# Grouped-query attention on one core: six of eight Q loads move from SyncE's queue to GpSimd's, in a pattern of outermost count 8

## The chip, the core and the metric

The kernel runs on one core of one Trainium2 chip. The core has a matmul engine (TensorE, PE in the profile), two elementwise engines (VectorE, DVE; ScalarE, ACT), GpSimd (POOL), a sequencer that mostly issues transfers (SyncE, SP), and 16 DMA engines that carry all transfers between the device's memory and the core's on-chip memory of 128 partitions. The metric is the device time of one execution in microseconds.

## The reference

```python
B, Hq, Hkv, Sq, Sk, D = 16, 32, 8, 16, 2048, 128        # all bf16
k = jnp.repeat(k, Hq // Hkv, axis=1)
v = jnp.repeat(v, Hq // Hkv, axis=1)
scores = jnp.einsum("bhqd,bhkd->bhqk", q, k) * D ** -0.5
p = _softmax(scores, axis=-1)
return jnp.einsum("bhqk,bhkd->bhqd", p, v)
```

Four query heads of 16 rows share one K/V head, so each of the 16 x 8 = 128 groups is a 64-row softmax attention over 2048 keys of length 128. K and V are 512 KB a group each, Q and the output 16 KB: nearly all bytes are K and V, and each is read once.

## The kernel before

**Tiling.** Two groups make a pair, so that 2 x 64 query rows fill the 128 partitions. There are NP = 64 pairs, and eight pairs make a Q chunk of 1024 rows (NQC = 8 chunks, 256 KB each). For each pair the kernel loads K (`load_k`, L163, 1 MB) and V (`load_v`, L170, 1 MB). VectorE transposes K in blocks (L291, two instructions a pair); TensorE forms the scores `S_ps` (L244); VectorE scales them into `Sneg` and takes the row minimum of the negated scores (L307); ScalarE takes the exponential into `P` with its row sum (L336); TensorE transposes `P` in two halves (L259) and ScalarE copies them out (L346); TensorE multiplies by V (L275, "PV"), and ScalarE scales by the reciprocal row sum (L356) into `Osb`, which is stored (`store`, L190).

**Q.** A chunk is loaded by `load_q` (L183) into one of NQ = 2 buffers `Qn`, with eight consecutive rows of Q in a partition: partition a holds rows 8a to 8a+7, 2 KB in a piece. TensorE transposes it in four parts (L227; the operation "QT" of its program), and ScalarE copies each part into `QT` (L326), where it also puts the 1024 columns back in the order of the rows: column 8a+j comes from partition a, place j. The four parts of chunk c+1 are placed in the programs behind pairs 8c+2 to 8c+5.

**Order and queues.** Every engine runs a list that is written out before (`pe_prog`, `act_prog`), with semaphores between engines. SP issues all transfers in one loop over t (L195): K of pair t, then Q of chunk c when t = max(0, 8c - QLEAD) with QLEAD = 7, then V of pair t - 4, then the output of pair t - 12. It waits for a free buffer before each: K has six buffers (`sem_kt`), V eight (`sem_pv`), and Q of chunk c waits (L186) until chunk c-2 has been transposed (`sem_st`). The last pair's V is loaded in two halves (L181), and the second half of its PV waits for the second. GpSimd only builds the two identity matrices at the start, which TensorE waits for.

Of the kernel before, what the change touches and what calls it, by code (L numbers as in the profile page):

```python
# [5 lines left out]
ACT = mybir.ActivationFunctionType  # L6
ALU = mybir.AluOpType
BF16 = mybir.dt.bfloat16
# [8 lines left out]
NQ = 2  # L17
# [4 lines left out]
QLEAD = 7  # L22


def bass_standalone__gqa_softmax__sampling_kernel(
# [14 lines left out]
    NQC = NP // 8  # L40
# [3 lines left out]
    sb = lambda name, shape, dt: ctx.enter_context(nc.sbuf_tensor(name, shape, dt))  # L44
# [6 lines left out]
    Vb = [sb(f"Vb{i}", [128, 2, J, 128], BF16) for i in range(NV)]  # L51
    KT = [sb(f"KT{i}", [128, 2, J * 64], F32) for i in range(NKT)]
    Qn = [sb(f"Qn{i}", [128, 8, 128], BF16) for i in range(NQ)]

    QT = [sb(f"QT{i}", [128, 4, 1024], BF16) for i in range(2)]
    Sneg = [sb(f"Sneg{i}", [128, Sk], F32) for i in range(2)]
# [16 lines left out]
    sem_q = [sem(f"sem_q{i}") for i in range(NQ)]  # L73
    sem_o = [sem(f"sem_o{i}") for i in range(NO)]
    sem_kt = sem("sem_kt")
    sem_max = sem("sem_max")
    sem_rec = sem("sem_rec")
    sem_s = sem("sem_s")
# [61 lines left out]
    def stage_ap(u):  # L140
        return ST_ps[:, 512 * (u % NSTAGE):512 * (u % NSTAGE + 1)]
# [7 lines left out]
    with nc.Block() as block:  # L149

        @block.gpsimd
        def _(gp):
            gp.iota(iota_t[:, :], [[1, 128]], base=0, channel_multiplier=-1).then_inc(sem_id, 1)
            gp.wait_ge(sem_id, 1)
            gp.tensor_scalar(ident[:, :], iota_t[:, :], 0.0, None, op0=ALU.is_equal).then_inc(sem_id, 1)  # L155
            gp.tensor_scalar(ident4[:, :], iota_t[:, :], 0.0, None, op0=ALU.is_equal).then_inc(sem_id, 1)

        @block.sync
        def _(sp):
            def load_k(p):  # L160
                s = p % NK
                if p >= NK:
                    sp.wait_ge(sem_kt, 2 * (p - NK) + 2)  # L163
                if p == 0:
                    for g in range(2):
                        sp.dma_start(Kn[s][:, g, :], kf[:, g, :]).then_inc(sem_k0[g], 16)  # L166
                else:
                    sp.dma_start(Kn[s][:, :, :], kf[:, 2 * p:2 * p + 2, :]).then_inc(sem_k[s], 16)  # L168

            def load_v(p):  # L170
                s = p % NV
                if p >= NV:
                    sp.wait_ge(sem_pv, p - NV + 1)
                if p < NP - 1:
                    dst = Vb[s][:, :, :, :].rearrange("a g j d -> a g (j d)")
                    sp.dma_start(dst, vf[:, 2 * p:2 * p + 2, :]).then_inc(sem_v[s], 16)  # L176
                    return
                for x in range(2):
                    dst = Vb[s][:, :, 8 * x:8 * (x + 1), :].rearrange("a g j d -> a g (j d)")
                    src = vf[:, 2 * p:2 * p + 2, 1024 * x:1024 * (x + 1)]  # L180
                    sp.dma_start(dst, src).then_inc(sem_vl[x], 16)  # L181

            def load_q(c):  # L183
                s = c % NQ
                if c >= NQ:
                    sp.wait_ge(sem_st, last_q[c - NQ, 3] + 1)  # L186
                src = qf[1024 * c:1024 * (c + 1), :].rearrange("(a j) d -> a j d", j=8)
                sp.dma_start(Qn[s][:, :, :], src).then_inc(sem_q[s], 16)

            def store(p):  # L190
                s = p % NO
                sp.wait_ge(sem_nm, p + 1)
                sp.dma_start(of[128 * p:128 * (p + 1), :], Osb[s][:, :]).then_inc(sem_o[s], 16)  # L193

            for t in range(NP + SLAG + 1):  # L195
                if t < NP:
                    load_k(t)
                for c in range(NQC):
                    if t == max(0, 8 * c - QLEAD):
                        load_q(c)  # L200
                if 0 <= t - VLAG < NP:
                    load_v(t - VLAG)
                if 0 <= t - SLAG < NP:
                    store(t - SLAG)
            for s in range(NO):
                sp.wait_ge(sem_o[s], 16 * (NP // NO))

        @block.tensor
        def _(pe):
            pe.wait_ge(sem_id, 3)  # L210

            def free(u):
                if u >= NSTAGE:
                    pe.wait_ge(sem_ev, u - NSTAGE + 1)

            for op in pe_prog:
                if op[0] == "QT":
                    _, c, i, u = op
                    if i == 0:
                        pe.wait_ge(sem_q[c % NQ], 16 * (c // NQ + 1))  # L220
                    free(u)
                    dst = stage_ap(u).bitcast(BF16)
                    src = Qn[c % NQ][:, :, :].rearrange("p j (b c e) -> p j b e c", b=2, e=2)
                    b, e = divmod(i, 2)
                    for j in range(8):
                        for r in range(4):
                            ins = pe.transpose(dst[32 * r:32 * (r + 1), 128 * j:128 * (j + 1)], src[:, j, b, e, :], ident[:, :])  # L227
                    ins.then_inc(sem_st, 1)
                elif op[0] == "S":
                    _, p = op  # L230
                    pe.wait_ge(sem_kt, 2 * p + 2)
                    if p >= 1:
                        pe.wait_ge(sem_max, p)
                    c, i = divmod(p, 8)
                    if i == 0:
                        pe.wait_ge(sem_ev, last_q[c, 3] + 1)
                    kt = KT[p % NKT][:, :, :].bitcast(BF16).rearrange("p g (t b x e) -> p g b e t x", t=J // 2, b=2, e=2)
                    qt = QT[c % 2]
                    for acc in range(4):
                        b, e = divmod(acc, 2)  # L240
                        for r in range(4):
                            rows = slice(32 * r, 32 * (r + 1))
                            for g in range(2):
                                ins = pe.matmul(  # L244
                                    S_ps[64 * g:64 * (g + 1), 512 * r:512 * (r + 1)],
                                    qt[rows, acc, 128 * i + 64 * g:128 * i + 64 * (g + 1)],
                                    kt[rows, g, b, e, :, :],
                                    start=(acc == 0), stop=(acc == 3),
                                )
                    ins.then_inc(sem_s, 1)  # L250
                elif op[0] == "PT":
                    _, p, h, u = op
                    if h == 0:
                        pe.wait_ge(sem_exp, p + 1)
                    free(u)
                    dst = stage_ap(u)
                    for t in range(4):
                        x = 4 * h + t
                        ins = pe.transpose(dst[:, 128 * t:128 * (t + 1)], P[p % 2][:, 128 * x:128 * (x + 1)], ident4[:, :])  # L259
                    ins.then_inc(sem_st, 1)  # L260
                elif op[0] == "PV":
                    _, p = op
                    pe.wait_ge(sem_ev, last_p[p, 1] + 1)
                    if p < NP - 1:
                        pe.wait_ge(sem_v[p % NV], 16 * (p // NV + 1))
                    if p >= NP - 3:
                        pe.wait_ge(sem_max, NP)
                    elif p >= 1:
                        pe.wait_ge(sem_nm, p)
                    pt = PT[p % NPT][:, :, :].bitcast(BF16).rearrange("p t (q e) -> p t e q", e=2)  # L270
                    for j in range(J):
                        if p == NP - 1 and j % 8 == 0:
                            pe.wait_ge(sem_vl[j // 8], 16)
                        for g in range(2):
                            ins = pe.matmul(  # L275
                                o_ap(p)[64 * g:64 * (g + 1), :],
                                pt[:, j // 2, j % 2, 64 * g:64 * (g + 1)],
                                Vb[p % NV][:, g, j, :],
                                start=(j == 0), stop=(j == J - 1),
                                skip_group_check=True,  # L280
                            )
                    ins.then_inc(sem_pv, 1)
# [36 lines left out]
        def _(act):  # L319
            for op in act_prog:  # L320
                if op[0] == "qe":
                    _, c, i, u = op
                    act.wait_ge(sem_st, u + 1)
                    if c >= 2 and i == 0:
                        act.wait_ge(sem_s, 8 * (c - 1))
                    act.activation(  # L326
                        QT[c % 2][:, i, :].rearrange("p (a j) -> p a j", j=8),
                        stage_ap(u).bitcast(BF16).rearrange("p (j a) -> p a j", j=8), ACT.Copy,
                    ).then_inc(sem_ev, 1)
                elif op[0] == "exp":  # L330
                    _, p = op
                    act.wait_ge(sem_max, p + 1)
# [53 lines left out]
```

## Time and profile before

| what | value |
|---|---|
| median of three timed runs | 353.08 us (351.69 to 353.13) |
| the profiled execution, its time | 352.63 us |
| its span, first to last instruction | 350.4 us |
| mean granted TensorE clock | 0.937 |
| read from device memory, written | 136.31 MB, 2.10 MB |
| mean rate over the span | 395 GB/s |

In the page, "busy" is the time in which an engine executed, and its share is of the span. The strip of slices cuts the span into 40 and gives a digit for tenths. A group of instructions shows its line, engine, operation, tiles and count, then busy us, the mean ns of one, the idle time of the engine before the group's instructions, and what ended that idle time. The queue lines give packets, megabytes and the time their packets took as a share of all 16 DMA engines' span; a queue of kind "instruction" carries the engines' programs. A line of the answer by stretches gives the stretch and its length, then the busy time and count of PE, PEld (TensorE's weight loads), DVE, ACT and POOL, then the granted clock, the DMA share and the GB/s.

### The profile page before, as it was taken

The page shows a single profiled execution, that of the slowest core. Times are in us where ns is not written, and L with a number is a line of the kernel's source. Part 1 is how long each engine was busy: PE and PEld are TensorE (multiplying, and loading weights), DVE is VectorE, ACT ScalarE, POOL GpSimd, SP SyncE. Part 2 cuts the span into 40 slices and gives each one's busy share as a digit, 9 for nine tenths or more (in the row PEclk, how much of TensorE's full clock was granted, in tenths as well). Part 3 has the DMA queues.
Part 4 walks back from the last instruction along what each step waited for, and adds up shares of the span by engine and source line. Part 5 has one row for each costly group of instructions (what it writes and reads, how often), then busy time and mean ns, then how long its engine had stood idle before and what let it go on. Part 6 is the DMA issues. An engine that isn't in the chain of part 4 may idle for free.

```text
span 350.4 us, 12631 instructions
## 1 busy us (share of the span) xinstructions
PE 243.3 (69%) x5632; PEld 173.5 (50%) x5632; DVE 296.3 (85%) x320; ACT 255.6 (73%) x353; POOL 1.4 (0%) x7
## 2 busy tenths in 40 slices
PE   2578876778667775687649666676775776697675
PEld 2246544546445543365436544454563554465454
DVE  2899999978789887889888897898888888988980
ACT  2578887877758785678757976578957689676575
POOL 1000000000000000000000000000000000000000
PEclk9769999998989999899998999899988999988899
DMA  7999999999999999999999999999999999999983
GB/s 280 416 408 409 406 408 405 412 411 408 414 410 410 412 409 411 410 413 408 408 412 411 409 412 408 410 415 406 411 412 410 410 389 410 412 411 411 409 342 117
DMA packets 45525, 139.22 MB, mean 397 GB/s; under 512 B 11424, under 2 KB 11424, under 8 KB 45472
## 3 DMA queue, kind: packets, MB, share of 16 engines
q1 hardware_dynamic: 45472, 138.42, 99.5%
q8 instruction: 44, 0.72, 0.8%
q14 instruction: 9, 0.07, 0.1%
HBM read 136.31 MB, written 2.10 MB: 395 GB/s over the span
## 4 chain that ended last, share of the span: by engine, by line
DMA 75%; DVE 10%; SPq 6%; issue 5%; PE 2%; ACT 1%
DMA Kn<-in_k_dram 70%; DVE KT L291 8%; DMA Vb<-in_v_dram 4%; SPq L176 3%; DVE Sneg L307 2%; SPq L193 2%; DMA Qn<-in_q_dram 1%; ACT QT L326 1%; SPq L168 1%; PE S_ps L244 1%; PE O_ps L275 0%; PE ST_ps L227 0%; SPq L181 0%; SPq L166 0%; ACT O L356 0%
## 5 line engine op out<-in xcount | busy, mean ns | idle before, releaser
L291 DVE STREAM_TRANSPOSE KT<-Kn 128x1024 f32<-128x1024 f32 x128 | 151.8, 1225 | 43.6 <-DMA Kn<-in_k_dram 43.5
L336 ACT ACTIVATE P<-Sneg,nbias 128x2048 bf16<-128x2048 f32 x64 | 128.1, 2001 | 37.4 <-DVE Sneg L307 37.0
L307 DVE TENSOR_SCALAR_CACHE_REDUCE Sneg<-S_ps 128x2048 f32<-128x2048 f32 x64 | 144.2, 2253 | 1.8 <-PE S_ps L244 1.8
L244 PE MATMUL S_ps<-KT,QT 32*64 32x512 bf16 x2048 | 81.3, 425 | 87.5 <-DVE Sneg L307 75.2
L244 PEld LDWEIGHTS S_ps<-KT,QT 32*64 32x64 bf16 x2048 | 33.7, 109 | 113.5 <-issue 102.7
L346 ACT ACTIVATE PT<-ST_ps 128x512 f32<-128x512 f32 x128 | 69.9, 596 | 21.4 <-PE ST_ps L259 21.4
L259 PE MATMUL ST_ps<-ident,P 128*128 128x128 f32 x512 | 73.1, 288 | 8.9 <-ACT P L336 8.6
L275 PEld LDWEIGHTS O_ps<-Vb,PT 128*64 128x64 bf16 x1952 | 63.1, 119 | 30.3 <-issue 28.8
L275 PE MATMUL O_ps<-Vb,PT 128*64 128x128 bf16 x1952 | 73.7, 233 | 1.2 <-issue 1.0
L259 PEld LDWEIGHTS ST_ps<-ident,P 128*128 128x128 f32 x512 | 57.5, 145 | 18.1 <-ACT P L336 13.6
L356 ACT ACTIVATE O<-O_ps,rrec 128x128 bf16<-128x128 f32 x61 | 22.3, 366 | 25.7 <-PE O_ps L275 25.0
L326 ACT ACTIVATE QT<-ST_ps 128x1024 bf16<-128x1024 bf16 x32 | 32.4, 1024 | 5.6 <-PE ST_ps L227 5.5
L227 PE MATMUL ST_ps<-ident,Qn 128*32 128x128 bf16 x1024 | 21.4, 233 | 6.4 <-DMA Qn<-in_q_dram 6.4
L227 PEld LDWEIGHTS ST_ps<-ident,Qn 128*32 128x32 bf16 x1024 | 16.3, 103 | 11.3 <-issue 10.9
L298 DVE RECIPROCAL rrec<-rowsum 128x1 f32<-128x1 f32 x64 | 10.1, 158 | 2.3 <-ACT P L336 2.3
L336 ACT ACTIVATION_READ_ACCUMULATOR P<-Sneg,nbias 128x1 f32 x64 | 12.1, 188 | 0.0
L307 DVE DVE_READ_ACCUMULATOR Sneg<-S_ps 128x1 f32 x64 | 5.3, 83 | 0.0
L275 PE MATMUL S_ps<-Vb,PT 128*64 128x128 bf16 x96 | 3.4, 220 | 0.7 <-DMA Vb<-in_v_dram 0.6
L275 PEld LDWEIGHTS S_ps<-Vb,PT 128*64 128x64 bf16 x96 | 2.9, 110 | 1.2 <-DMA Vb<-in_v_dram 0.7
L356 ACT ACTIVATE O<-S_ps,rrec 128x128 bf16<-128x128 f32 x3 | 1.1, 369 | 2.0 <-PE S_ps L275 2.0
L326 ACT ACT_TABLE_LOAD x1 | 1.3, 1283 | 0.7 <-PEq L371 0.7
L155 POOL TENSOR_SCALAR ident<-iota_t 128x128 bf16<-128x128 int32 x1 | 0.5, 534 | 0.1
(6 smaller groups left out, 1.2 us busy)
## 6 DMA issues: line engine op xcount, KB each, us to landing
Kn<-in_k_dram SPq DMA_DIRECT2D x63, 1024.0 KB, 15.0
Vb<-in_v_dram SPq DMA_DIRECT2D x63, 1024.0 KB, 16.3
Qn<-in_q_dram SPq DMA_DIRECT2D x8, 256.0 KB, 14.6
out_dram<-O SPq DMA_DIRECT2D x64, 32.0 KB, 13.9
Kn<-in_k_dram SPq DMA_DIRECT2D x2, 512.0 KB, 4.1
Vb<-in_v_dram SPq DMA_DIRECT2D x2, 512.0 KB, 13.4
```

The source lines that it names most:

```text
L176: sp.dma_start(dst, vf[:, 2 * p:2 * p + 2, :]).then_inc(sem_v[s], 16)
L227: ins = pe.transpose(dst[32 * r:32 * (r + 1), 128 * j:128 * (j + 1)], src[:, j, b, e, :], ident[:, :])
L244: ins = pe.matmul(S_ps[64 * g:64 * (g + 1), 512 * r:512 * (r + 1)], qt[rows, acc, 128 * i + 64 * g:128 * i + 64 * (g + 1)], kt[rows, g, b, ...
L259: ins = pe.transpose(dst[:, 128 * t:128 * (t + 1)], P[p % 2][:, 128 * x:128 * (x + 1)], ident4[:, :])
L275: ins = pe.matmul(o_ap(p)[64 * g:64 * (g + 1), :], pt[:, j // 2, j % 2, 64 * g:64 * (g + 1)], Vb[p % NV][:, g, j, :], start=(j == 0), stop ...
L291: dve.transpose(KT[p % NKT][:, g, :].rearrange("p (t b a e) -> p t e b a", t=J // 2, b=2, e=2), Kn[p % NK][:, g, :].bitcast(F32).rearrange ...
L298: dve.reciprocal(rrec[:, p:p + 1], rowsum[:, p:p + 1]).then_inc(sem_rec, 1)
L307: dve.tensor_scalar(Sneg[p % 2][:, :], S_ps[:, :], -scale, None, op0=ALU.mult, op1=ALU.min, accum_out=nbias[:, p:p + 1],).then_inc(sem_max, 1)
L326: act.activation(QT[c % 2][:, i, :].rearrange("p (a j) -> p a j", j=8), stage_ap(u).bitcast(BF16).rearrange("p (j a) -> p a j", j=8), ACT. ...
L336: act.activation(P[p % 2][:, :].bitcast(BF16).rearrange("p (t r x) -> p t r x", t=8, r=4), Sneg[p % 2][:, :].rearrange("p (r t x) -> p t r ...
L346: act.activation(PT[p % NPT][:, 4 * h:4 * (h + 1), :].rearrange("p t q -> p (t q)"), stage_ap(u), ACT.Copy,).then_inc(sem_ev, 1)
L356: act.activation(Osb[p % NO][:, :], o_ap(p), ACT.Copy, scale=rrec[:, p:p + 1]).then_inc(sem_nm, 1)
```

## The change

The loads of Q chunks 1 to 6 are issued by GpSimd instead of SP; chunks 0 and 7 stay on SP where they were. The source is viewed as (y x j) with x = 8 and j = 8, and x is outermost, so partition 16x + y holds rows 8(8y + x) to 8(8y + x) + 7 of the chunk, again 2 KB in a piece. Ahead of each of these six loads GpSimd issues a transfer of 16 pieces of 16 elements into a new tile `turn` that nothing reads, its source also with 8 outermost. The loads count on their own semaphores `sem_qs`; chunk c still waits until chunk c-2 has been transposed. ScalarE's copy into `QT` reads the 1024 columns in another order for these chunks, so that `QT` holds the same as before.

```diff
+    turn = sb("turn", [16, NQC, 16], BF16)
...
+    sem_turn = sem("sem_turn")
+    sem_qs = [sem(f"sem_qs{i}") for i in range(NQ)]
...
             gp.tensor_scalar(ident4[:, :], iota_t[:, :], 0.0, None, op0=ALU.is_equal).then_inc(sem_id, 1)
+            for c in range(1, NQC - 1):
+                if c >= NQ:
+                    gp.wait_ge(sem_st, last_q[c - NQ, 3] + 1)
+                few = qf[16 * c:16 * (c + 1), 0:16].rearrange("(y x) d -> x y d", x=8)
+                gp.dma_start(turn[:, c, :], few).then_inc(sem_turn, 16)
+                src = qf[1024 * c:1024 * (c + 1), :].rearrange("(y x j) d -> x y (j d)", x=8, j=8)
+                gp.dma_start(Qn[c % NQ][:, :, :], src).then_inc(sem_qs[c % NQ], 16)
+            gp.wait_ge(sem_turn, 16 * (NQC - 2))
...
-                    if t == max(0, 8 * c - QLEAD):
+                    if c in (0, NQC - 1) and t == max(0, 8 * c - QLEAD):
                         load_q(c)
...
-                        pe.wait_ge(sem_q[c % NQ], 16 * (c // NQ + 1))
+                        if c in (0, NQC - 1):
+                            pe.wait_ge(sem_q[c % NQ], 16)
+                        else:
+                            pe.wait_ge(sem_qs[c % NQ], 16 * ((c + 1) // NQ))
...
-                    act.activation(
-                        QT[c % 2][:, i, :].rearrange("p (a j) -> p a j", j=8),
-                        stage_ap(u).bitcast(BF16).rearrange("p (j a) -> p a j", j=8), ACT.Copy,
-                    ).then_inc(sem_ev, 1)
+                    if 0 < c < NQC - 1:
+                        dst = QT[c % 2][:, i, :].rearrange("p (y x j) -> p y x j", x=8, j=8)
+                        src = stage_ap(u).bitcast(BF16).rearrange("p (j x y) -> p y x j", j=8, x=8)
+                    else:
+                        dst = QT[c % 2][:, i, :].rearrange("p (a j) -> p a j", j=8)
+                        src = stage_ap(u).bitcast(BF16).rearrange("p (j a) -> p a j", j=8)
+                    act.activation(dst, src, ACT.Copy).then_inc(sem_ev, 1)
```

## The prediction

> **What bounds the kernel now.** I read the engines' busy shares first, then the strip of slices, then the DMA queues, then the chain that ended last, and last the end of the run in short stretches. The first four, from the page of the kernel before:
>
> ```profile
> PE 243.3 (69%) x5632; PEld 173.5 (50%) x5632; DVE 296.3 (85%) x320; ACT 255.6 (73%) x353; POOL 1.4 (0%) x7
> ...
> DMA  7999999999999999999999999999999999999983
> ...
> q1 hardware_dynamic: 45472, 138.42, 99.5%
> q8 instruction: 44, 0.72, 0.8%
> q14 instruction: 9, 0.07, 0.1%
> ...
> DMA 75%; DVE 10%; SPq 6%; issue 5%; PE 2%; ACT 1%
> ...
> L291 DVE STREAM_TRANSPOSE KT<-Kn 128x1024 f32<-128x1024 f32 x128 | 151.8, 1225 | 43.6 <-DMA Kn<-in_k_dram 43.5
> ```
>
> No compute engine is full: VectorE is busiest at 85%, and nearly all that it waits for before L291 is the next K tile. The transfers are full from the first slice to the last but two, and are 75% of the chain. So what counts is when the slowest of the 16 DMA engines has done its share of 138 MB. The end shows that they don't finish together; rows are stretches, with DMA share and GB/s last:
>
> ```profile
> 325.00:335.00 10.00, 7.01 (x141) 4.60 (x139) 9.00 (x11) 6.62 (x9) 0.00 (x0) 0.83 1.03 406
> 335.00:339.00 4.00, 2.02 (x44) 1.32 (x40) 3.00 (x4) 2.49 (x4) 0.00 (x0) 1.00 0.99 381
> 339.00:343.00 4.00, 4.00 (x111) 3.60 (x104) 2.38 (x3) 3.60 (x6) 0.00 (x0) 1.00 0.64 235
> 343.00:347.40 4.40, 2.99 (x66) 2.37 (x61) 0.17 (x1) 2.87 (x7) 0.00 (x0) 1.00 0.46 147
> 347.40:350.40 3.00, 0.61 (x16) 0.45 (x16) 0.00 (x0) 0.37 (x1) 0.00 (x0) 1.00 0.10 23
> ```
>
> From 339 us on about half of the DMA engines are done, and the other half works on for 8 us. The trace also keeps the time of each of the 16 increments by which a load counts as landed, one per DMA engine. For the last half V tile eight stand at 338.77 to 339.98 us (0 to 1.21 after the first) and eight at 345.26 to 347.33 (6.50 to 8.57 after it). The spread grows steadily: at most 1.8 us for the load landing at 25 us, 4.1 at 121, 7.3 at 210. The increments carry no engine's name, but the set is always a group of eight light and a group of eight late.
>
> Queue 8 is what makes them late. Its 0.72 MB are the instructions of TensorE (5632 loads and 5632 matmuls of 64 bytes), in 44 packets of 16 KB. 0.8% of 16 engines' 350.4 us is 44.9 us, or 1.02 us each; the 4 KB packet behind one takes 0.44 us in the packet records where 0.16 is usual. So a fetch costs its engine some 1.3 us, and the 43 fetches up to 339 us, over eight engines, cost 43 x 1.3 / 8 = 7.0 us each. The mean of the late group less that of the light one is 7.25 - 0.62 = 6.6 us.
>
> **The change, part by part.** *Q leaves SP's queue.* Six transfers (c = 1 to 6) of 128 rows of 2 KB were spread over 16 DMA engines, 8 rows each; the packet records have 0.084 us for a 2 KB row. Every engine loses 6 x 8 x 0.084 = 4.03 us. SP also loses six issues (median 2.08 us in the group of L188) and most of the 5.9 us that it waits there for L227 (c = 7 stays on SP with its wait). K, V and output issues behind them go out that much sooner, which gains nothing: a K or V load lands 15 to 16 us after its issue, so it queues at the engines:
>
> ```profile
> Kn<-in_k_dram SPq DMA_DIRECT2D x63, 1024.0 KB, 15.0
> Vb<-in_v_dram SPq DMA_DIRECT2D x63, 1024.0 KB, 16.3
> Qn<-in_q_dram SPq DMA_DIRECT2D x8, 256.0 KB, 14.6
> ```
>
> *Q comes back on GpSimd's queue.* With 8 as the outermost count I expect each load on eight DMA engines, 16 rows each: 6 x 16 x 0.084 = 8.06 us for a receiver, or +4.03 net, and -4.03 for the other eight. The tiny transfer of the same count moves the starting engine on by eight, so that all six Q loads fall on the same eight. The trace of before has no transfer from GpSimd, so which eight is not to be read from it. That the receivers are the light group is an assumption, and the largest in this forecast.
>
> The Trainium skill, page "DMA: Bandwidth & Descriptors", section "Why a DMA increments its semaphore by 16 and not by 1", states that a DMA is split over the largest number up to 16 that divides the slowest dimension of both patterns, and that from GpSimd, when that is under 16, consecutive engines are taken from a cursor that goes round; no run here shows it yet. The same page's "Rules for kernel authors" speak against the change: an outermost count under 16 confines a DMA to that many engines, so put a multiple of 16 outermost. By that rule alone, which takes the engines as equal, the receivers would set the end and the time would be 352.63 + 4.03 = 356.7; the 0.64 and 0.46 of the stretches after 339 us say that they are not equal.
>
> *Sum, receivers light.* The last half V tile: late group 347.33 - 4.03 = 343.3; light group 339.98 + 4.03 = 344.0, which now is last. *Alternating two queues on a receiver* may cost more than bytes. Below: 0, as the 256-byte output rows between K's rows cost only their 18 ns. Above: one 8 KB packet of queue 14, at 172 us, set two light engines back by 0.35 and 0.52 us where 8 KB of K's rows take 0.32, so 0.03 to 0.20 per change of queue. Once per row at the lower figure that is 96 x 0.03 = 2.9 us, once per load at 0.1 us it is 0.6. I take 0.6, since a whole stream waits behind the first row and can be fetched ahead, and keep 0 and 2.9. So V lands at 344.6, 2.7 us earlier. The last K tile moves from 325.13 + 8.22 = 333.3 to 325.13 + 1.86 + 4.03 + 0.6 = 331.6, 1.7 us earlier; the work behind it (L291, L307, L336, L259, L346, half of L275) ended at 346.1, so it ends at 344.4 and V is still last. What follows V is as before: L275 0.64, L356 0.37, the store, and 350.4 to 352.63 outside the span. 352.63 - 2.7 = 349.9.
>
> *Tiny transfers.* 16 pieces of 32 bytes on eight engines, below the 18 ns of a 256-byte row: 6 x 2 x 0.018 = 0.2 us at most, on the other eight, which have 0.7 us to spare. *Later Q* costs nothing: GpSimd issues c = 1 at about 2.2 us, behind ident4, and PE reads it at 27.4; c = 2 can go at 10.0 and is read at 63.7; c = 3 at 42.3 and 107.1. Behind each wait on GpSimd there are only further Q loads, and PE's wait has 25 us and more of cover. The Trainium skill, page "SBUF — State Buffer", section "Who interferes with whom", warns that a VectorE instruction in a two-port mode keeps GpSimd from writing its descriptors; L307 takes 2253 ns for 2048 elements and L291 1225 for 1024, over 1 ns an element, which doesn't look like a fast mode, and such a delay would have to exceed 25 us to matter. *The new order in L326* (24 of 32): L336 walks three dimensions at 0.98 ns an element, L326 takes 1.00 now, so 0. Were each to double to 2.05 us, ACT's 255.6/64 = 4.0 us per pair would be 5.0 in four pairs of eight, under the 5.2 us that a pair's 2 MB take. The three timed runs have a median 0.45 us over the profiled one, so 349.9 is 350.4 beside the 353.08.
>
> **The rivals.** *A, the receivers are the late group* (ends slower). They get +4.03 on top of 8.57: V lands at 351.4, the time is 356.7, or 357.1 beside the median. For it: nothing in the trace ties light to either half. Against: only that both halves are possible. It decides by one bit, where the starting engine stands; if the six were split evenly over both halves nothing would change. *B, the switch between queues eats the gain.* The light group has 347.33 - 344.0 = 3.3 us, so it is gone at 3.3 / 96 = 35 ns a row; at 0.03 the time is 352.63 - 3.3 + 2.9 = 352.2 and at 0.2 a row 352.63 + 19.2 - 3.3 = 368. For it: 0.44 after a fetch; against: 0.03 was one packet, not a stream. *C, the change doesn't do what it says*: each Q load still goes over 16 DMA engines. Then each engine has the same bytes as before and the time is 352.6, 353.1 beside the median, the two groups still 6.6 us apart.
>
> **How the numbers follow.** Receivers light: 0.66; of these, by the switch's price, 0.54 are a gain of over 0.5% (about what a measurement here can tell from no change), 0.08 within it, 0.04 slower, the last two being B. Receivers late: 0.24, slower. C: 0.10, of which 0.08 within 0.5% and 0.02 slower by a fixed cost of the new queue. Faster 0.54, same 0.16, slower 0.30. The likeliest case's own range, beside the median, is 349.3 (no switch cost, 349.8, less 0.5 for the measurement) to 352.7 (2.9 of it). The whole range reaches down to 348.9, since single runs lie up to 1.4 under their median, and up to rival A, 357.2, as leaving A out would leave out more than 2 in 10.
>
> **What would show it.** Right: the DMA share stays near 1 until about 343 us and falls at once; the 16 increments of the last V load lie within 2 us instead of 8.6; L291's 43.6 us of idle time shrinks by some 2; the Q rows stand under a queue of GpSimd's with 6 x 128 rows. Under A the stretch at half share grows to 16 us; under B the light group's increments come last, later than 344.6; under C the spread stays at 8.6. The prediction is wrong if PE ever waits for Qn after 27 us, or if GpSimd's issues add time at either end of the span.

## The result, and the profile after

The changed kernel takes 365.11 us (median, 364.77 to 366.31) where the kernel before takes 353.11 on the same chip (351.69 to 353.60). The ratio is 1.035, with a 95% interval of 1.032 to 1.038. It is 12 us slower; the forecast was 350.4 and the range ended at 357.2. The profiled execution has a span of 363.0 us, 12.6 more than before.

These lines are from the page of the changed kernel: the DMA share by slices, the GB/s of the same 40 slices (9.1 us each), the queues, the chain by engine, the largest group on VectorE, and the issues of GpSimd.

```profile
DMA  7999999999999999999999999999999999999993
GB/s 261 331 367 408 409 321 403 411 411 407 353 410 411 413 409 339 393 397 415 408 330 382 413 411 410 409 400 403 410 408 413 405 409 400 409 411 409 410 328 96
...
q1 hardware_dynamic: 44608, 136.85, 97.6%
q0 software_dynamic: 1056, 1.58, 1.9%
q8 instruction: 44, 0.72, 0.8%
...
DMA 77%; DVE 12%; SPq 4%; issue 3%; PE 3%; ACT 0%
...
L305 DVE STREAM_TRANSPOSE KT<-Kn 128x1024 f32<-128x1024 f32 x128 | 151.9, 1226 | 56.8 <-DMA Kn<-in_k_dram 56.7
...
Qn<-in_q_dram POOLq DMA_DIRECT2D x6, 256.0 KB, 9.3
...
turn<-in_q_dram POOLq DMA_DIRECT2D x6, 0.5 KB, 5.8
```

The bound is the same one. VectorE's transposes took 151.8 us before and 151.9 now, but the idle time before them grew from 43.6 to 56.8 us, and K's transfers end all of it. The DMA share is as full as before, so a share alone would tell nothing. The rate tells it. This is the same strip before:

```profile
GB/s 280 416 408 409 406 408 405 412 411 408 414 410 410 412 409 411 410 413 408 408 412 411 409 412 408 410 415 406 411 412 410 410 389 410 412 411 411 409 342 117
```

There, no slice but the first and the last two is under 389 GB/s. Now the rate dips in five places, and each is a Q load that GpSimd issued (at 2.9, 11.9, 45.4, 90.1, 133.8 and 177.9 us; the first two share a dip). Against 408 GB/s the slices of the dips lack 464 GB/s x 9.075 us, or 10.3 us of transfer at the full rate.

Here is one such place in the changed kernel, in stretches of 2 us with the DMA share and the GB/s last:

```profile
46.00:48.00 2.00, 0.94 (x25) 0.78 (x21) 2.00 (x2) 1.87 (x3) 0.02 (x1) 1.00 1.03 403
48.00:50.00 2.00, 1.66 (x39) 1.00 (x37) 1.32 (x4) 1.64 (x3) 0.00 (x0) 1.00 1.09 385
50.00:52.00 2.00, 1.74 (x45) 1.45 (x38) 2.00 (x2) 1.68 (x3) 0.00 (x0) 1.00 1.02 217
52.00:54.00 2.00, 0.57 (x6) 0.33 (x4) 2.00 (x2) 1.08 (x2) 0.00 (x0) 1.00 1.02 242
54.00:56.00 2.00, 1.53 (x47) 0.91 (x49) 0.39 (x3) 1.65 (x1) 0.00 (x0) 1.00 1.03 377
```

And the same place in the kernel before, where the rate never moves:

```profile
50.00:52.00 2.00, 1.03 (x35) 0.53 (x33) 2.00 (x4) 1.83 (x3) 0.00 (x0) 1.00 1.02 403
52.00:54.00 2.00, 2.00 (x54) 1.61 (x39) 2.00 (x3) 1.61 (x3) 0.00 (x0) 1.00 1.02 403
```

For 4 us the DMA engines move 54 to 60% of the bytes while they count as fully busy. If eight engines only carried Q's rows instead of K's, no rate would fall. The packet records say what happens: the 4 KB packets of SP's queue, which carry K and V and have nothing to do with Q, take 0.24 to 0.33 us from 50 to 54 us (medians of half microseconds) where 0.159 is usual. Extra rows on eight engines would lengthen their queues, but not the packets of the other eight; here 99% of these packets take over 0.18 us, where 1% do in the same stretch before. So all 16 engines are slowed. In what follows, this is called the stall, and what it does to the rate a dip.

The end, in stretches of the changed kernel:

```profile
345.00:349.00 4.00, 2.82 (x71) 2.17 (x72) 3.68 (x6) 2.82 (x5) 0.00 (x0) 1.00 1.03 353
349.00:353.00 4.00, 2.19 (x66) 1.40 (x65) 2.75 (x4) 2.99 (x4) 0.00 (x0) 1.00 0.94 333
353.00:357.00 4.00, 3.20 (x82) 2.77 (x76) 1.70 (x4) 3.60 (x8) 0.00 (x0) 1.00 0.46 168
357.00:360.00 3.00, 2.58 (x58) 2.26 (x58) 0.15 (x1) 1.93 (x5) 0.00 (x0) 1.00 0.34 94
360.00:363.00 3.00, 0.61 (x16) 0.45 (x16) 0.00 (x0) 0.37 (x1) 0.00 (x0) 1.00 0.11 24
```

The stage at half share, 353 to 360 us, is still there and about as long as before (339 to 347), but emptier: 0.46 and 0.34, where it was 0.64 and 0.46. For the last half V tile, the increments stand at 352.55 us and 0 to 1.19 after it (ten), and 4.95 to 7.38 after it (six); before it was eight and eight. Its last one comes at 359.93, against 347.33: 12.6 us later, which is the whole difference of the spans. Both groups moved, the first increment by 13.8.

### The profile page after: what moved, and what is told of

It is laid out like the page before. It is cut to its first block, busy times and chain, and to the rows that moved or that the text cites. A ratio compares the mean times of both kernels' runs of the same rounds, so it can differ in the third digit from the quotient of the medians.

```text
span 363.0 us, 12638 instructions
## 1 busy us (share of the span) xinstructions
PE 252.1 (69%) x5632; PEld 178.9 (49%) x5632; DVE 296.8 (82%) x320; ACT 254.6 (70%) x353; POOL 8.6 (2%) x19
## 4 chain that ended last, share of the span: by engine, by line
DMA 77%; DVE 12%; SPq 4%; issue 3%; PE 3%; ACT 0%
DMA Kn<-in_k_dram 74%; DVE KT L305 7%; DVE Sneg L321 4%; DMA Vb<-in_v_dram 3%; SPq L187 2%; PE S_ps L258 1%; PE O_ps L289 1%; SPq L204 1%; SPq L192 1%; SPq L177 0%; SPq L179 0%; PE S_ps L289 0%; SPq L199 0%; DVE rrec L312 0%; ACT O L373 0%
## 5 line engine op out<-in xcount | busy, mean ns | idle before, releaser
L305 DVE STREAM_TRANSPOSE KT<-Kn 128x1024 f32<-128x1024 f32 x128 | 151.9, 1226 | 56.8 <-DMA Kn<-in_k_dram 56.7
L258 PE MATMUL S_ps<-KT,QT 32*64 32x512 bf16 x2048 | 84.5, 437 | 87.5 <-DVE Sneg L321 78.0
L273 PE MATMUL ST_ps<-ident,P 128*128 128x128 f32 x512 | 74.8, 292 | 11.4 <-ACT P L353 11.0
L289 PEld LDWEIGHTS O_ps<-Vb,PT 128*64 128x64 bf16 x1952 | 66.2, 123 | 31.8 <-issue 28.8
L289 PE MATMUL O_ps<-Vb,PT 128*64 128x128 bf16 x1952 | 77.2, 240 | 1.5 <-issue 1.5
L273 PEld LDWEIGHTS ST_ps<-ident,P 128*128 128x128 f32 x512 | 59.3, 149 | 21.7 <-ACT P L353 17.2
L346 ACT ACTIVATE QT<-ST_ps 128x1024 bf16<-128x1024 bf16 x32 | 32.4, 1025 | 7.0 <-PE ST_ps L241 7.0
L241 PEld LDWEIGHTS ST_ps<-ident,Qn 128*32 128x32 bf16 x1024 | 16.3, 103 | 12.6 <-issue 12.6
L312 DVE RECIPROCAL rrec<-rowsum 128x1 f32<-128x1 f32 x64 | 10.2, 159 | 2.3 <-ACT P L353 2.3
L164 POOL DMA_DIRECT2D turn<-in_q_dram x6 | 3.5, 582 | 169.1 <-PE ST_ps L241 169.1
L166 POOL DMA_DIRECT2D Qn<-in_q_dram x6 | 3.7, 624 | 0.0
```

The source lines that it names most:

```text
L258: ins = pe.matmul(S_ps[64 * g:64 * (g + 1), 512 * r:512 * (r + 1)], qt[rows, acc, 128 * i + 64 * g:128 * i + 64 * (g + 1)], kt[rows, g, b, ...
L289: ins = pe.matmul(o_ap(p)[64 * g:64 * (g + 1), :], pt[:, j // 2, j % 2, 64 * g:64 * (g + 1)], Vb[p % NV][:, g, j, :], start=(j == 0), stop ...
L305: dve.transpose(KT[p % NKT][:, g, :].rearrange("p (t b a e) -> p t e b a", t=J // 2, b=2, e=2), Kn[p % NK][:, g, :].bitcast(F32).rearrange ...
L312: dve.reciprocal(rrec[:, p:p + 1], rowsum[:, p:p + 1]).then_inc(sem_rec, 1)
L346: act.activation(dst, src, ACT.Copy).then_inc(sem_ev, 1)
```

## The experiments

The expectations use these names. QUEUE: the second queue, or GpSimd's issuing, costs the time. LATE: the receivers are the late group, and their bytes cost it. OWN: a plain load gives each DMA engine partitions that no other engine writes; the pattern of 8 breaks this, and all engines stall. SIX-TWO: of the eight engines that fetch TensorE's instructions, six lie in the half that GpSimd's Q loads fall on and two in the other. Further names are explained in the expectation that uses them. "Pattern of 8" and "pattern of 16" stand for the number of outer steps in the source. The diffs are excerpts, and "..." marks what is left out: conditions, semaphore counts, and ScalarE's copy where it follows the new order.

**The queue alone.** GpSimd issues Q in the old pattern of 128 rows, with no tiny transfer; ScalarE's copy is as before. Against the kernel before:

```diff
+            for c in range(1, NQC - 1):
+                if c >= NQ:
+                    gp.wait_ge(sem_st, last_q[c - NQ, 3] + 1)
+                src = qf[1024 * c:1024 * (c + 1), :].rearrange("(a j) d -> a j d", j=8)
+                gp.dma_start(Qn[c % NQ][:, :, :], src).then_inc(sem_qs[c % NQ], 16)
...
```

> The six Q loads come from GpSimd, but in SyncE's old pattern (row blocks a, then j), whose outermost count is 128, and with no tiny transfer. In the changed kernel all 16 DMA engines run at 55 to 60% of their rate for some 4.5 us at each of the six Q loads, about 1.5 to 1.9 us lost per load. Theory QUEUE (the stretches come from a second queue beside SyncE's, or from GpSimd's way of issuing): the six dips stay, the time is 353 + 6 x 1.5 to 1.9 = 362 to 364. Theory PATTERN (they come from eight engines writing 8 blocks of 16 partitions): no dips, the time is 353 (within 1), since every engine has the bytes that it had.

**The pattern alone.** SP issues Q, where it did before, in the pattern of 8.

```diff
                 src = qf[1024 * c:1024 * (c + 1), :].rearrange("(a j) d -> a j d", j=8)
+                if 0 < c < NQC - 1:
+                    src = qf[1024 * c:1024 * (c + 1), :].rearrange("(y x j) d -> x y (j d)", x=8, j=8)
                 sp.dma_start(Qn[s][:, :, :], src).then_inc(sem_q[s], 16)
...
```

> All Q loads stay on SyncE's queue, but those of chunks 1 to 6 take the source pattern with 8 outermost; GpSimd issues nothing. Theory PATTERN: the dips are there, 1.5 us each, and 353 + 9 = 362, with 4 more or less as the eight engines are the late or the light ones. Theory QUEUE: no dips; if the eight engines are the late ones 353 + 4 = 357, if the light ones 353 - 3 = 350. The 16 completion increments of the last V tile show which: a spread of 8.6 + 8 = 16.6 us (or what the buffers allow, some 8.5) for late receivers, about 2 for light ones.

The queue alone takes 352.23 us against 352.40 (ratio 0.999, 0.996 to 1.002); the pattern alone takes 364.89 (1.035, 1.030 to 1.039). The GB/s strip and GpSimd's queue of the first:

```profile
GB/s 278 411 408 407 407 404 407 412 411 411 410 410 413 408 409 410 413 412 408 409 412 410 412 411 410 411 415 406 410 411 412 409 403 408 412 411 410 397 351 119
...
q0 software_dynamic: 480, 1.57, 1.2%
```

The same strip of the second:

```profile
GB/s 288 365 410 409 386 366 406 411 411 365 381 410 413 411 351 382 410 412 407 344 396 409 411 394 337 397 412 410 409 410 404 405 412 408 411 413 408 391 272 41
```

The second queue carries all six loads and leaves no mark; without it, the pattern makes the same dips. So QUEUE falls, and with it the term of the sum for alternating two queues. What is wrong lies in the pattern. The Trainium skill, page "DMA: Bandwidth & Descriptors", section "Rules for kernel authors", says that spreading transfers over several issuing engines adds no bandwidth, as all use the same 16 DMA engines; the 0.999 agrees.

**The tiny transfer.** In one run it stands behind each Q load and not ahead of it, so that the Q loads start from the other eight engines, if it does move the start by eight (this diff is against the changed kernel). In another it is added to the kernel before, and Q stays on SP.

```diff
-                gp.dma_start(turn[:, c, :], few).then_inc(sem_turn, 16)
...
                 gp.dma_start(Qn[c % NQ][:, :, :], src).then_inc(sem_qs[c % NQ], 16)
+                gp.dma_start(turn[:, c, :], few).then_inc(sem_turn, 16)
```

> The changed kernel with each tiny transfer issued behind its Q load instead of ahead of it, so that the Q loads should start eight engines further on. Theory LATE (the changed kernel gave the Q loads to the eight engines that also fetch TensorE's instructions): each late engine now loses 0.67 us per Q load instead of gaining 0.67, 6 x 1.34 = 8.1 us in all, of which the light engines' own new share lets some 6 to 8 be seen: 357 to 359, and the spread of the last V tile's increments falls from 7.4 us to under 4. If the changed kernel already had the light ones, this one is 4 to 8 slower: 369 to 373. If the starting engine plays no part: 365.

> The kernel before, with only the six tiny transfers added on GpSimd at the same points; all Q loads stay on SyncE. Theory QUEUE in its strong form (any transfer from GpSimd stalls the engines): dips at six points, over 1 us each, 359 or more. Theories PATTERN and LATE, and QUEUE where the stall goes by the bytes: 353 within 0.5.

The other half takes 364.84 us (1.034, 1.030 to 1.038), the tiny transfers alone 352.29 (1.000, 0.998 to 1.003). So the tiny transfers cost nothing, and the choice of the half hardly matters. LATE, which put the other half at 357 to 359, falls as the cause of the whole 12 us. The time alone is what was expected if the starting engine played no part (365). But the halves do differ in the increments of the last V load. With the tiny transfer behind, and in SP's pattern of 8, 14 stand within 2.0 us and two are 6.3 to 7.3 us late. In the changed kernel it was ten and six; at 200 us already, ten stand within 3.2 us and six are 7.0 to 8.0 late. So the tiny transfer does what it says, and the eight late engines are not one half: the numbers fit six in one half and two in the other.

**Source or destination.** SP loads Q in 8 outer steps, but each step reads 32 KB in one piece.

```diff
+                    src = qf[1024 * c:1024 * c + 1088, :].rearrange("(x y j) d -> x y (j d)", x=8, j=8)[:, 0:16, :]
...
```

> As the run with the pattern of 8 on SyncE, but each of the eight outer steps reads 16 neighbouring rows of 2 KB (a block of 32 KB, the blocks 34 KB apart so that they stay eight) in place of every eighth row; the on-chip side is the same, partitions 16x to 16x+15. The blocks reach 12 KB into the next chunk, so Q holds other rows than the reference asks for in these six chunks; bytes and counts are the same. Theory SOURCE (the eight engines in step read eight neighbouring rows, one 16 KB stretch of device memory at a time, and all engines stall on it): no dips, and the eight engines' extra 0.67 us per load falls on the light ones: 350 (349.5 to 352), the increments of the last V tile within 2 us. Theory DESTINATION (the eight engines in step write partitions y, 16+y, 32+y ...): dips as before, 363 to 366.

It takes 364.86 us (1.034, 1.029 to 1.039), and the dip at the load of chunk 2 is there (issued at 30.5 us, its data landing from 46.5 to 49.1):

```profile
44.00:46.00 2.00, 1.99 (x64) 1.19 (x53) 2.00 (x2) 2.00 (x3) 0.00 (x0) 1.00 1.07 258
46.00:48.00 2.00, 0.96 (x8) 0.86 (x8) 2.00 (x4) 1.51 (x4) 0.00 (x0) 1.00 1.01 314
```

For the pattern of 8, the order in device memory is not it. Next, the same on all 16 engines, once with strided and once with contiguous source blocks. Receivers and others are then the same engines, and nothing is moved between them.

```diff
+                    src = qf[1024 * c:1024 * (c + 1), :].rearrange("(y x j) d -> x y (j d)", x=16, j=8)
...
```

> All Q loads on SyncE, chunks 1 to 6 with 16 outermost in the source instead of 8, so that all 16 engines carry them, engine x reading rows x, x+16, ... of 2 KB, and writing eight partitions each. Theory SOURCE: 16 engines in step read one 32 KB stretch at a time; dips remain, 359 to 366. Theory DESTINATION, if it is the blocks of 16 partitions: no dips, 353 within 1, as every engine has the bytes that it had. Theory EIGHT (it is the crowding on eight engines itself, not either side's addresses): 353 too.

```diff
+                    src = qf[1024 * c:1024 * c + 1152, :].rearrange("(x y j) d -> x y (j d)", x=16, j=8)[:, 0:8, :]
...
```

> As the run with 16 outermost on SyncE, but each outer step reads eight neighbouring rows (a block of 16 KB, the blocks 18 KB apart so that they stay sixteen); Q of these six chunks holds other rows than asked for. On chip step x writes partitions 8x to 8x+7 as there. Theory DESTINATION (what stalls is that an engine writes partitions that it doesn't write in the plain pattern of 128 rows): the same dips, 359 to 361. If it was the source's order that stalled the strided run: no dips, 352 to 353.

They take 360.45 us (1.023, 1.019 to 1.028) and 361.11 (1.023, 1.019 to 1.028). The first falls in the range that SOURCE gave, the second does not (352 to 353), so it is not the source with 16 outer steps either. The strided run's other forecasts, 353 for EIGHT and for a stall that comes from blocks of 16 partitions, missed. The strip of the strided one:

```profile
GB/s 281 399 407 408 376 389 405 412 412 361 401 411 411 410 360 409 412 413 407 346 410 410 412 412 335 411 411 411 411 409 409 414 406 411 410 413 408 393 335 96
```

Every engine gets the bytes that it got before, the two groups of increments are as before (eight within 0.7 us, eight 5.5 to 7.2 behind), and yet there are five dips and 8.5 us more. Both groups moved: at the last V load the first increment comes 7.3 us later than before (346.07) and the last one 5.9 (353.27). This is the stall by itself: a cost of all engines, 1.0 to 1.4 us a load (5.9 and 8.5 us over six), that has nothing to do with who is late. What is left of the pattern is which engine writes which partitions. The same page's "Rules for kernel authors" say to put a multiple of 16 outermost in order to use all 16 engines, ideally the 128 partitions. These two runs have 16 outermost in the source and are slow, so the number of engines is not the whole of it. Its section "The descriptor swizzle" states that in a plain load of 128 partitions one engine writes partitions 0 to 3 and 32 to 35, the next 4 to 7 and 36 to 39, and so on, the lower 64 partitions by the lower eight engines, and that each engine thus writes one port. In the patterns of 8 and 16, an outer step is 16 or 8 neighbouring partitions, which by that section belong to two to four engines. The packet records name no engine, so no trace here shows this map itself; the last pair of runs below tests what follows from it.

**Engines kept to their own partitions.** In the first pair of runs each Q load is four transfers of 32 partitions with 8 outer steps of four partitions, on SP and on GpSimd (there each behind a tiny transfer). By the section's map, with SP's eight engines taken as the lower ones, half of the rows fall on own partitions, the other half on those of the other eight engines.

```diff
+                    src = qf[1024 * c:1024 * (c + 1), :].rearrange("(y w j) d -> w y (j d)", w=32, j=8)
+                    for b in range(4):
+                        sp.dma_start(Qn[s][32 * b:32 * (b + 1), :, :], src[8 * b:8 * (b + 1), :, :]).then_inc(sem_q[s], 16)
...
```

> All Q loads on SyncE. Each load of chunks 1 to 6 is cut into four transfers of 32 partitions, each with 8 outermost in the source: outer step x writes partitions 32b+4x to 32b+4x+3, so that the eight engines in step are 4 partitions apart, in place of 16 (the changed kernel) or 8 (the run with 16 outermost); the eight rows read in step are neighbours, as in the changed kernel. Theory SPREAD (the stall comes from engines in step writing partitions that share a way into the on-chip memory, which repeat at a distance of 16 and 8 partitions but not of 4): no dips, and the eight engines, light ones by the two earlier runs that began with them, take 0.67 us more per load and the late ones 0.67 less: 350 (349.5 to 352), the last V tile's increments within 3 us. Theory EIGHT (crowding on eight engines stalls them all, whatever the addresses): 362 to 366.

> The changed kernel with the same cut: four transfers of 32 partitions per Q load from GpSimd, each behind its own tiny transfer (24 of them). Theories SPREAD and LATE together: no dips; the receivers are the same eight as in the changed kernel, the late ones, which take 0.67 us more per load: 353 + 4 = 357 (355 to 359), the last V tile's spread 8.5 us or more. If the receivers are the light ones: 350, spread under 3. Theory EIGHT, or a stall that comes with GpSimd and eight engines: 362 to 366.

SP's takes 363.44 us (1.030, 1.028 to 1.033), GpSimd's 359.87 (1.022, 1.020 to 1.025). SPREAD, which forecast no dips, falls. EIGHT, which had missed with 16 outer steps, gave 362 to 366 here; SP's run meets that and GpSimd's does not. The dips are shallower: at chunk 2 SP's version has

```profile
44.00:46.00 2.00, 1.36 (x48) 0.92 (x32) 2.00 (x2) 2.00 (x2) 0.00 (x0) 1.00 1.09 289
46.00:48.00 2.00, 1.58 (x32) 1.22 (x37) 2.00 (x4) 1.51 (x5) 0.00 (x0) 1.00 0.98 359
```

which lacks 2 x (116 + 46) KB against 405 GB/s, 0.8 us, where the plain pattern of 8 on SP lacks 1.3 in its three stretches from 44 us (277, 276 and 389). That is the direction that OWN expects, but not proof. Why SP's and GpSimd's versions differ by 3.6 us was not found.

The decisive pair writes nothing but own partitions: five loads (chunks 2 to 6), of which half goes to the receivers' 64 partitions of `Qn` and half to the same 64 of a spare tile that nothing reads, so bytes and rows per engine and load are as in the change.

```diff
...
+                        dst = (Qn if b < 2 else spare)[s][32 * (b % 2):32 * (b % 2 + 1), :, :]
+                        sp.dma_start(dst, src[8 * b:8 * (b + 1), :, :]).then_inc(sem_q[s], 16)
...
```

> From chunk 2 to 6 (five loads) each load is four transfers of 32 partitions with 8 outermost, as in the spread run, but all four write partitions 0 to 63 only: two into Q, two into a spare tile. Q's partitions 64 to 127 keep an older chunk's rows, so the result is another; bytes are the same. All on SyncE, so on the eight engines that it fills first. Theory OWN (each engine has partitions that only it writes in a plain 128-row transfer, for these eight all below 64; a write into another's partitions stalls both): no dips at all, where the spread run had one of 1.5 us or more per load. Theory SIX-TWO (of the eight late engines two are among these eight receivers and six among the others): two increments of the last V tile stand 9 to 12 us behind the first, the other 14 within some 5; 353 + 3 = 356 (355 to 358). Theory HALF (all eight late engines are the others): 350, all within 3 us.

```diff
...
+                    dst = (Qn if b < 2 else spare)[c % NQ][64 + 32 * (b % 2):96 + 32 * (b % 2), :, :]
+                    gp.dma_start(turn[:, 4 * c + b, :], few).then_inc(sem_turn, 16)
+                    gp.dma_start(dst, src[8 * b:8 * (b + 1), :, :]).then_inc(sem_qs[c % NQ], 16)
...
```

> The mirror image: five loads from GpSimd, each of four transfers of 32 partitions behind a tiny transfer, which start on the other eight engines as in the changed kernel, and write partitions 64 to 127 only (two into Q, two into a spare tile; Q's partitions 0 to 63 keep an older chunk's rows, so the result is another). Theory OWN: no dips. SIX-TWO: six increments of the last V tile stand 8 us or more behind the first, two in between at 3 to 5, eight light; 353 + 3 = 356 (355 to 358). HALF: eight late, none in between, 356 too.

They take 355.22 us (1.008, 1.006 to 1.010) and 355.77 (1.009, 1.007 to 1.012) against 352.60. SP's on partitions 0 to 63: the strip, and the end.

```profile
GB/s 289 415 408 408 407 408 405 410 412 407 410 413 411 412 408 411 409 412 397 407 412 411 411 392 392 414 413 408 410 413 410 411 409 410 407 412 408 391 308 44
```

```profile
345.00:348.00 3.00, 2.19 (x61) 2.03 (x56) 0.17 (x1) 2.77 (x6) 0.00 (x0) 1.00 0.16 57
348.00:350.00 2.00, 2.00 (x66) 1.83 (x66) 0.00 (x0) 1.42 (x3) 0.00 (x0) 1.00 0.26 68
```

GpSimd's on partitions 64 to 127, the same stretches:

```profile
345.00:348.00 3.00, 2.84 (x72) 2.51 (x71) 0.79 (x3) 2.79 (x4) 0.00 (x0) 1.00 0.42 157
348.00:350.00 2.00, 1.35 (x20) 1.19 (x22) 0.17 (x1) 1.77 (x6) 0.00 (x0) 1.00 0.36 100
```

The dips are gone: no slice between the second and the 37th is under 392 in SP's (384 in GpSimd's), where the changed kernel goes down to 321. The bytes and rows of a load, the eight engines, the four transfers and the queues are those of the first pair; the partitions that two of the four write are what differs (and that these two go to a spare tile). With 355 us EIGHT falls for good. So OWN holds: the stall comes from engines that write outside the partitions which the plain loads give them. No run writes other engines' partitions only, which would be the opposite test. What it is in the chip, the port that the page names or something else, no run here shows.

The ends of the two show the halves. From 345 to 348 us a DMA share of 0.16 is two or three engines of 16, and 0.42 is six or seven. The increments of the last V load agree: SP's has 14 within 2.7 us and two at 7.1 and 7.4; GpSimd's has ten within 1.6 us and six at 6.1 to 7.9. SIX-TWO holds by these counts. Its distances do not: SP's two late ones were expected 9 to 12 us behind, and GpSimd's run should have had two in between at 3 to 5 us. The traces show a limit: from 240 us on the widest spread of a K or V load in any 40 us lies between 8 and 10 us in every run, the kernel before included, wherever Q went. So bytes put on late engines show in the time and not in the spread; why the spread stops there was not tested. Either way some receivers were already late, and 5 x 16 x 0.084 x 1/2 = 3.4 us more of Q on them is near what the two medians lost, 2.6 and 3.2 us.

The two costs, measured apart, come near the change. The stall alone (16 outermost) is 8.5 us, the late receivers alone (own partitions) 2.6 and 3.2 us for five loads, so 3.1 and 3.8 for six: 11.6 to 12.3 together. The change cost 12.0. How it divides is not shown, though, as the 8.5 us belong to another pattern: its slices under 400 GB/s lack 6.4 us of transfer against 408, where those of the changed kernel lack 10.2. By its own dips the stall is some 10 of the 12 us. It is the larger part either way.

**A better version?** If bytes are to go to light engines only, output stores can do it: they only read on-chip memory. Every fifth store goes out in transfers of 124 and 4 partitions.

```diff
...
+                if p % 5:
+                    sp.dma_start(of[128 * p:128 * (p + 1), :], Osb[s][:, :]).then_inc(sem_o[s], 16)
+                    return
+                sp.dma_start(of[128 * p:128 * p + 124, :], Osb[s][0:124, :]).then_inc(sem_o[s], 16)
+                sp.dma_start(of[128 * p + 124:128 * (p + 1), :], Osb[s][124:128, :]).then_inc(sem_o[s], 16)
...
```

> This leaves the Q loads as in the kernel before. Every fifth output store (13 of 64) goes out in two transfers, of 124 and of 4 partitions, both of which divide by 4 and by no larger number up to 16 that the other does too; on SP I expect each on the first four engines. A store only reads on-chip memory, so by the theory of own partitions nothing stalls. A 256-byte row takes 0.018 us in the packet records of the kernel before; 12 of these stores lie ahead of the last V load. Every other engine loses 12 x 8 x 0.018 = 1.7 us, the four gain 3 x 1.7 = 5.2. If the first four engines hold none of the two late ones of their half: the late engines end at 347.33 - 1.7 = 345.6 and the four at 339.98 + 5.2 = 345.2, so the kernel is about 1.7 us faster, ratio 0.995. If one or both of the late are among the first four: they end at 347.33 + 5.2 = 352.5, ratio 1.015, with one or two increments of the last V load standing alone. If stores in part of the engines stall all 16 as well, the time rises in both cases and GB/s dips every fifth pair.

It takes 351.66 us against 352.02 (0.999, 0.997 to 1.001): no difference that can be told, where 0.995 was expected. The issues on its page:

```profile
out_dram<-O SPq DMA_DIRECT2D x51, 32.0 KB
...
out_dram<-O SPq DMA_DIRECT2D x13, 31.0 KB
out_dram<-O SPq DMA_DIRECT2D x13, 1.0 KB
```

In the one trace the increments moved as meant, but by about half of it. A split store has ten records, eight of which come with its data: four engines for each of its two transfers (the other two come at once, one for each). At the last V load the eight late engines end at 346.40 us (347.33 before), and of the light eight, four stand within 0.4 us, two at 1.6 to 2.0 and two at 4.7 to 5.0. So it looks as if the first four engines hold none of the late ones; the late eight gained 0.9 of the 1.7 us expected, and there is no dip (a store is an eighth of a Q load, so a dip would be small). That is too little to be told from nothing in the time, and no version here is shown to beat the kernel before.

## Why the prediction was wrong, step by step

- *The transfers bound the kernel, and the slowest DMA engine sets the end.* Right: the last V increment moved by 12.6 us and the span by 12.6.
- *Instruction fetches make eight engines late.* Right in size: a group of eight, 5 to 8 us behind, is in every run that leaves the shares of bytes alone. What ties it to the fetches is the sum in the prediction and the trace of before, where one increment steps from 6.3 to 7.4 us behind the first between the loads that begin to land at 202 and at 204 us, and a fetch starts at 203.2. No run changes the number of fetches, so the cause is argued. Wrong in place: I took the eight for one half ("a group of eight light and a group of eight late"); they are six of one half and two of the other.
- *Eight receivers, the same eight each time.* Right: the increments separate by the half chosen, and moving the tiny transfer behind the load changes the half.
- *"That the receivers are the light group is an assumption."* It failed, and so does the other value of it: neither half is light. Rival A had the mechanism for this half, and without the stall about its size too: 355.8 us was measured for five loads where it gave 357.1 for six. The measured 365.1 is not A's.
- *+4.03 us for a receiver and -4.03 for the other eight.* This is the step that failed most. The sum took a Q load to cost its rows on the engines that carry them, and nothing on the others. The load stalls all 16 engines, receivers or not: instead of 343.3 us for the late group and 344.0 for the light one, the increments of the last V load end at 353.7 (ten) and 359.9 (six). The stall is 8.5 us in the pattern of 16 and some 10 by the dips of the changed kernel, of 12.0.
- *"Alternating two queues on a receiver may cost more than bytes"*, 0.6 us, 0 to 2.9. This was the only place in the sum for an extra cost, and it is none: a second queue costs nothing (0.999). I looked for the cost on the receivers, and bounded it by one 8 KB packet. Nothing in my sum, and no rival, held a price for 16 engines at once; B would have reached 368, but for another reason and on eight engines only. The page of before could not show it, as every load there is of 128 rows; what it did offer was the `rearrange` of the diff, whose partitions I counted (16 rows for a receiver) but did not compare with those of a plain load.
- *Later Q, the tiny transfers and ScalarE's new order cost nothing.* Right. Six tiny transfers alone are 1.000; ScalarE's copies into `QT` have the same mean (L326, 1024 ns before; L346, 1025 now); PE waits for Qn once, at the start; GpSimd is busy for 8.6 us in all and nothing waits for it.
- *"The DMA share stays near 1"* as what would show the forecast right: it did stay (0.94 or more up to 353 us) while the rate fell to 217 GB/s at a share of 1.02. It was the wrong column to name; a stalled engine counted as busy here.

## What to carry to other kernels

Where transfers bound a kernel, as here, an access pattern decides not only how many DMA engines carry a load, but which partitions each of them writes. Keep the 128-partition load plain, or cut it so that each engine stays in the partitions that the other loads give it, and look for the effect in GB/s by slices, not in the DMA share. Before moving bytes from late to light engines, find out which engines are late by steering a small load and reading the 16 increments; here the late ones lay in both halves.

## What was not expected

- Six loads of 256 KB, 1.1% of the bytes, slow the transfers of all others: 4 KB packets of K and V take 0.21 to 0.33 us (medians of half microseconds) where 0.159 is usual, for some 4 us a load.
- The stall needs no partial use of the engines: 16 outer steps on 16 engines cost 8.5 us.
- GpSimd's queue is free here: 1.57 MB in 480 packets beside a full stream on SP's gave 0.999.
- On SP a load on eight engines leaves nine records of its semaphore, one at once and eight with the data; GpSimd's leaves 16. The Trainium skill, page "DMA: Bandwidth & Descriptors", section "Why a DMA increments its semaphore by 16 and not by 1", states this difference of the two paths, and the records agree.
